# Linear attention and a squared-ReLU FFN in one kernel: the first batch's loads and its second group of rows, arranged anew

## The chip, the cores and the metric

The kernel runs on one core of a Trainium2 chip, in one launch. The metric is the device time of that launch in microseconds. The kernel before took 202.36 us in the median of three runs (202.26 to 202.84).

The core has five engines that run their own instructions in order and wait for each other by semaphores: TensorE (PE; its weight loads are shown apart as PEld), VectorE (DVE), ScalarE (ACT), GpSimd (POOL) and SyncE (SP, which issues most of the DMAs here; ACT issues a few). The DMAs of both queues run on the core's 16 DMA engines.

## The reference, cut to what matters

```python
# q, k, v: (4 batches, 4 heads, 1088 rows, 32); S1, S2: (8, 32); w_in: (128, 2048); w_out: (2048, 128)
def phi(x):                       # 64 features of a row: the outer product of two projections
    a = einsum('rd,bhsd->bhsr', S1, x)
    b = einsum('rd,bhsd->bhsr', S2, x)
    return einsum('bhsi,bhsj->bhsij', a, b).reshape(..., 64)
q_p, k_p = phi(q), phi(k)
kv  = einsum('bhsf,bhsd->bhfd', k_p, v)
z   = sum(k_p, axis=2)
num = einsum('bhsf,bhfd->bhsd', q_p, kv)
den = einsum('bhsf,bhf->bhs', q_p, z)[..., None] + 1e-06
x   = (num / den).transpose(0, 2, 1, 3).reshape(4352, 128)     # 4 heads side by side
out = maximum(x @ w_in, 0) ** 2 @ w_out                        # (4352, 128), float32
```

## The kernel before

**Tiling.** A batch has 1088 rows a head. A head's rows are laid over 32 partitions, 34 rows to a partition; the four heads of q or k fill the 128 partitions. The first 8 rows of 34 make tiles of group 0 and 1 (four tiles each), the last 2 rows are "the rest". v is laid the other way: partition 32 i + n holds rows 34 n + 8 i to 34 n + 8 i + 7, and the four heads stand side by side in the free dimension (256 numbers each), with a column of ones behind them. `load_v(b, i, eng)` fills 32 partitions (block i of rows) for all heads; four of them load a batch. `load_v_rest` loads the rest.

**The attention.** `turned` transposes q or k in 32 x 32 blocks on DVE; `proj` multiplies by S1 and S2 on PE and ACT copies the result out of PSUM; `outer` makes the 64 features of a row on DVE or POOL. `Kv` sums k's features times v over all rows (32 products of 128 rows and 4 of the rest) and `finish` copies the sums into the block-diagonal tile kvbd. `feature_t` transposes q's features on PE (t_ps) and copies them out (phT). `numerators` multiplies them by kvbd (nd). `normalize` divides on DVE by the denominators, scales each row for float16, transposes it on PE (x_ps) and has ACT copy it to xT: one chunk of 512 rows. Batches 1 to 3 go another way for some of this (`proj4`, `factors_gen`, `features_gen`, `KvRows`), where q's projections are written to a scratch in HBM (q_rows) and read back spread out (f, L285 and L290).

**The FFN.** Per chunk of 512 rows there are 16 blocks. A block multiplies xT by 128 columns of w_in (pg, L857), takes max(.,0) (gt) and squares it (g) on DVE, ACT and POOL, and multiplies by w_out (po, L944). `first_product` issues the first half some three blocks ahead of the second. There are 8 chunks, and a ninth of 256 rows made of the rests, whose products (po and po_r, L903) are made row block by row block; `rows_store` scales and stores them.

**Order.** The schedule is written by hand: instructions stand on each engine in the order in which the program issues them. The last part of the function, from the first `idle_products(6)` to `add_work`, is the first stretch: it makes chunk 0 and part of chunk 1 in straight line. After it a loop issues one block at a time, and between blocks `pump` lets generators ("lanes") issue pieces of the attention of later chunks: `x_gen` (numerators and normalization), `batch_gen`, `second_gen`. `now` counts blocks. `take_nd` and `nd_taken` guard the one PSUM buffer nd. Later loads are issued from a list by block number.

**PSUM buffers** are tagged: ms, pg and po have two buffers each, nd one. `idle_products` are products of zeros on PE, with no use of their result.

**DMA issue.** In the program's order, SP loads k's two groups and rest, q's group 0 (`load_group`), v (four `load_v`), q's group 1, w_in, w_out and then batch 1. Eight semaphores serve the DMAs in turn, so that an issue waits until the DMA eight places ahead of it has landed.

Of the kernel before, what the change touches and what calls it, by code (L numbers as in the profile page):

```python
# [21 lines left out]
def kernel(  # L22
# [86 lines left out]

    def load_v(b, i, eng):  # L110
        eng.dma_start(
            _v(v_sb[b], 0, [[256, H], [1, 256]], 32 * i, 32),
            bass.AP(
                v.tensor,
                v.offset + (b * H * S + 8 * i) * D,
                [[NM * D, 32], [S * D, H], [1, 256]],
            ),
        )

# [84 lines left out]
    own_j = cpool.tile([128, 16], F32)  # L204

    def sum_constants():
        dve.tensor_reduce(
            out=pick_s[:, :], in_=_v(iden, 0, [[1, 32], [32, 4]]), axis=AX, op=add
        )
        dve.tensor_copy(  # L210
            out=_v(pick, 0, [[8, 32], [1, 8]]), in_=_v(pick_s, 0, [[1, 32], [0, 8]])
        )
        dve.tensor_reduce(
            out=_v(own_j, 0, [[8, 2], [1, 8]]),
            in_=_v(iden, 0, [[64, 2], [1, 8], [8, 8]]),
            axis=AX,
            op=add,
        )
# [290 lines left out]
            )  # L509
        return nd  # L510

    def normalize(nd, T, xT, col, parts=1):

        small = [apool.tile([128, 16], F32, name=f"small{i}", tag=f"small{i}") for i in range(5)]
        den, rden, top, rtop, rs = small
        mm = apool.tile([128, 4], F32, tag="mm")
        mp = apool.tile([128, 4], F32, tag="mp")
        rm = apool.tile([128, 4], F32, tag="rm")
        beta = apool.tile([128, 4], F32, tag="beta", bufs=4)
        xs = apool.tile([128, 512], F16, tag="xs")  # L520
        num = _v(nd, 0, [[256, T], [VW, 4], [1, 32]])
        dve.tensor_scalar(
            out=den[:, 0 : 4 * T], in0=_v(nd, D, [[256, T], [VW, 4]]),
            scalar1=1e-6, scalar2=None, op0=add,
        )
        dve.reciprocal(rden[:, 0 : 4 * T], den[:, 0 : 4 * T])
        dve.tensor_reduce(
            out=_v(top, 0, [[4, T], [1, 4]]), in_=num,
            axis=AX, op=amax, apply_absolute_value=True,
        )  # L530
        yield 1, 1
        dve.tensor_tensor(
            out=rtop[:, 0 : 4 * T], in0=top[:, 0 : 4 * T], in1=rden[:, 0 : 4 * T], op=mult
        )
        dve.tensor_reduce(
            out=mm[:, 0:T], in_=_v(rtop, 0, [[4, T], [1, 4]]),
            axis=AX, op=amax, apply_absolute_value=True,
        )
        dve.tensor_scalar(  # L539
            out=mp[:, 0:T], in0=mm[:, 0:T], scalar1=1.0, scalar2=1.0 / 1024.0,  # L540
            op0=add, op1=mult,
        )
        dve.reciprocal(rm[:, 0:T], mp[:, 0:T])
        if parts == 1:
            dve.tensor_tensor(
                out=_v(rs, 0, [[4, T], [1, 4]]),
                in0=_v(rden, 0, [[4, T], [1, 4]]),
                in1=_v(rm, 0, [[1, T], [0, 4]]),
                op=mult,
            )  # L550
            yield 1, 1
            dve.tensor_tensor(
                out=_v(xs, 0, [[128, T], [32, 4], [1, 32]]),
                in0=_v(nd, 0, [[256, T], [VW, 4], [1, 32]]),
                in1=_v(rs, 0, [[4, T], [1, 4], [0, 32]]),
                op=mult,
            )
        else:
            yield 1, 1
            for i in range(T):  # L560
                dve.scalar_tensor_tensor(
                    out=_v(xs, 128 * i, [[32, 4], [1, 32]]),
                    in0=_v(nd, 256 * i, [[VW, 4], [1, 32]]),
                    scalar=rm[:, i : i + 1],
                    in1=_v(rden, 4 * i, [[1, 4], [0, 32]]),
                    op0=mult,
                    op1=mult,
                )
        pool.tensor_tensor(  # L569
            out=beta[:, 0:T], in0=mp[:, 0:T], in1=mp[:, 0:T], op=mult  # L570
        )
        yield 2, 0
        m = T if parts == 1 else 2
        for i in range(0, T, m):
            ms_used()
            x_ps = pspool.tile([128, 512], F16, name="x_ps", tag="ms", bufs=2)
            for t in range(i, i + m):
                nc.tensor.transpose(
                    x_ps[:, 128 * t : 128 * t + 128],
                    xs[:, 128 * t : 128 * t + 128],  # L580
                    iden16[:, :],
                )
            act.copy(
                xT[:, col + 128 * i : col + 128 * (i + m)], x_ps[:, 128 * i : 128 * (i + m)]
            )
        return beta
# [49 lines left out]
            yield 1, 0  # L636
        nd_taken[0] = True

    def x_gen(b, g, phT, rests=()):

        yield from take_nd()
        while pool_free[0] > now[0] + 0.6 and not hurry[0]:
            yield 1, 0
        nd = numerators(b, phT)
        quiet[0] = now[0] + 3
        yield 1, 1
        xT = apool.tile([128, 512], F16, name="xT", tag="xT", bufs=3)
        norm = normalize(nd, 4, xT, 0)
        yield next(norm)
        yield next(norm)  # L650
        next(norm)
        yield 1, 0
        nd_taken[0] = False
        for u in rests:
            rest_numerators(u)
        yield 1, 0
        yield from ms_one()
        beta = yield from norm
        chunk_of(b, g, xT, beta)
# [76 lines left out]
        if b % 2 == 1:  # L736
            add_work(rest_x(b // 2))

    def first_gen(phT):
        yield from x_gen(0, 1, phT)  # L740

    xT_rem = cpool.tile([128, 256], F16)
    rem_beta, rem_dst = [], []
    nd_rem, phT_rem = {}, {}
# [28 lines left out]
    def rest_x(r):  # L773
        beta = yield from normalize(nd_rem[r], 1, xT_rem, 128 * r)
        rem_beta.append((beta, 1))
        for w in range(2):
            for i in range(2):
                dst = bass.AP(
                    out.tensor,
                    out.offset + ((2 * r + w) * S + 32 + i) * E,  # L780
                    [[NM * E, 32], [1, E]],
                )
                rem_dst.append((dst, 64 * w + 32 * i, 32, 128 * r, 128))
        if r == 1:
            chunks[2 * B] = (xT_rem, 2, rem_beta, rem_dst)

# [124 lines left out]
    def rows_store(r, ci):  # L911
        beta, _ = chunks[ci][2][r]
        o_sb = fpool.tile([128, 128], F32, name="o_row", tag="o_row", bufs=2)
        dve.tensor_tensor(
            out=o_sb[:, :],
            in0=po[r][:, 0:128],
            in1=_v(beta, 0, [[0, 128]]),
            op=mult,
        )
        for i, (dst, p0, n, _, w) in enumerate(chunks[ci][3][4 * r : 4 * r + 4]):  # L920
            (sp, act)[i % 2].dma_start(dst, _v(o_sb, 0, [[1, w]], p0, n))

    def block():
        while len(stream) <= LOOK and first_product():
# [5 lines left out]
        if nt < 512:  # L930
            if c == 0:
                po[1] = pspool.tile([128, 512], F32, name="po_r", tag="ms", bufs=2)
            rows_product(c, 0, g2)
            if c < NC - 3:
                rows_product(c, 1, g2)
            else:
                held.append((c, 1, g2))
# [29 lines left out]
    xk += [turned(k_sb[0], g) for g in (1, 2)]  # L967
    pk = [proj(xk[0], "pg"), proj(xk[1], "pg")]
    proj_rests([(xk[2], 0, "k")])
    phk = [ph_tile("ph_k", 3) for g in range(2)]  # L970
    phq = ph_tile("ph_q", 2)
    for g in range(2):
        outer(phk[g], pk[g][1], 0, 2, dve, pk[g][0])
        outer(phk[g], pk[g][1], 2, 2, pool)
    xq = turned(q_sb[0], 0)
    idle_products(4)
    pq = proj(xq)
    outer_rest(0, "k", dve)
    outer(phq, pq[1], 0, 2, dve, pq[0])
    outer(phq, pq[1], 2, 1, dve, pq[0])  # L980
    outer(phq, pq[1], 3, 1, pool)
    xq1 = turned(q_sb[0], 1)
    sum_constants()
    kv0 = Kv(0)
    for g in range(2):
        kv0.tiles(phk[g], g, range(4))
    kv0.rest()
    kv0.finish((act, act))
    pqT = [feature_t(phq, 4, pr, (act, dve)[pr]) for pr in range(2)]
    nd0 = numerators(0, pqT, True)  # L990
    pq1 = proj(xq1, "pg")
    phq1 = ph_tile("ph_q", 2)
    for c in range(3):
        act.copy(
            w_in[:, 512 * c : 512 * c + 512], w_in32[:, 512 * c : 512 * c + 512]
        )
    idle_products(12)
    xT0 = apool.tile([128, 512], F16, name="xT", tag="xT", bufs=3)
    norm = normalize(nd0, 4, xT0, 0, 4)
    for _ in range(3):  # L1000
        next(norm)
    for t0 in (0, 2):
        outer(phq1, pq1[1], t0, 2, dve)
    try:
        next(norm)
    except StopIteration as done:
        chunk_of(0, 0, xT0, done.value)
    first_two()
    pqT1 = [feature_t(phq1, 4, pr, None) for pr in range(2)]
    for _ in range(2):  # L1010
        first_product()
    for pr in range(2):
        act.copy(pqT1[pr][0][:, :], pqT1[pr][1][:, :])
    act.copy(w_in[:, 1536:2048], w_in32[:, 1536:2048])

    lanes.append([first_gen([x[0] for x in pqT1]), 3, 1])
    add_work(*(batch_gen(b) for b in range(1, B)))
    later = []  # L1020
    for b in range(2, B):
# [45 lines left out]
```

## Time and profile before

| what | us |
|---|---|
| median of 3 runs | 202.36 |
| the profiled execution, its whole time | 202.01 |
| its span (first to last instruction) | 200.2 |
| PE busy | 193.0 |
| DVE busy | 121.9 |
| ACT busy | 109.4 |
| POOL busy | 62.7 |
| start of the first product with w_in (L886) | 17.86 |
| start of the first product with w_out (L944) | 19.68 |
| start of the last o_row on DVE (L914) | 196.80 |

The profile is of one execution. An engine's busy time is the time under its instructions; matmuls overlap in the pipeline, so PE's is not time at its peak. The chain of waits is followed back from the last instruction, at each step to what released it. "L245" is line 245 of the kernel before; tile names stand as output<-input. A window's row gives, for a stretch from A to B, the length, the busy us of PE, PEld, DVE, ACT and POOL with the instructions in brackets, the granted TensorE clock, the DMA share and GB/s.

### The profile page before, as it was taken

How to read it: one execution, taken by the hardware profiler on the slowest of the kernel's cores; microseconds unless marked ns; L12 is line 12 of the kernel's file. 1: busy time of each engine (PE TensorE's matmuls, PEld its weight loads, DVE VectorE, ACT ScalarE, POOL GpSimd, SP SyncE). 2: the span in 40 equal slices, each digit the busy share in tenths (PEclk: the TensorE clock that was granted, in tenths of full speed). 3: DMA queues.
4: the chain of work that ended last, by engine and by line, in shares of the span. 5: the costliest groups of instructions: out<-in, count | busy, mean ns of one | idle time of the engine just before them, and what ended most of it. 6: DMA issues, size and time to landing. Idle time of an engine off the chain costs nothing.

```text
span 200.2 us, 3760 instructions
## 1 busy us (share of the span) xinstructions
PE 193.0 (96%) x1416; PEld 102.8 (51%) x1416; DVE 121.9 (61%) x271; ACT 109.4 (55%) x216; POOL 62.7 (31%) x82
## 2 busy tenths in 40 slices
PE   7798999999999999999999999999999999999992
PEld 2575455455445464564346555454455444444792
DVE  4768694644994717459966573648456844544671
ACT  2236757544565566354674554555647565565570
POOL 3502220844262207441262254331332222223000
PEclk9999999999999999999999999999999999999999
DMA  5999720488300245782000117501000200100021
GB/s 159 279 356 246 229 47 0 137 188 211 111 0 0 66 153 164 210 246 81 2 3 0 52 58 222 194 3 54 0 0 3 52 0 0 38 16 0 3 52 26
DMA packets 14994, 18.34 MB, mean 92 GB/s; under 512 B 3072, under 2 KB 9472, under 8 KB 14976
## 3 DMA queue, kind: packets, MB, share of 16 engines
q1 hardware_dynamic: 14416, 18.00, 32.1%
q8 instruction: 11, 0.18, 0.4%
q10 hardware_dynamic: 560, 0.11, 0.3%
q14 instruction: 7, 0.06, 0.1%
HBM read 15.08 MB, written 3.01 MB: 90 GB/s over the span
## 4 chain that ended last, share of the span: by engine, by line
PE 86%; DVE 6%; DMA 4%; issue 1%; ACT 1%; SPq 0%; DVEq 0%
PE po L944 50%; PE pg L857 15%; PE nd L245 5%; DVE gt L873 2%; DMA v_sb<-in_v_dram 2%; PE kvr_ps L412 2%; PE o_ps L823 2%; PE ab_ps L245 2%; DMA k_sb<-in_k_dram 2%; PE po_r L903 2%; PE po L903 2%; PE idle_ps L224 1%; PE ab_ps L262 1%; PE kv_ps L375 1%; DVE ph_k L321 1%
## 5 line engine op out<-in xcount | busy, mean ns | idle before, releaser
L944 PE MATMUL po<-g,w_o 128*128 128x512 f32 x256 | 130.7, 592 | 0.0
L873 DVE TENSOR_SCALAR gt<-pg 128x512 f32<-128x512 f32 (+1 forms) x108 | 69.1, 646 | 51.7 <-PE pg L857 40.5
L876 ACT ACTIVATE g<-gt 128x512 f32<-128x512 f32 (+1 forms) x108 | 64.2, 599 | 66.0 <-DVE gt L873 63.7
L944 PEld LDWEIGHTS po<-g,w_o 128*128 128x128 f32 x256 | 48.5, 191 | 35.6 <-issue 21.3
L865 POOL TENSOR_TENSOR g<-gt 128x512 f32<-128x512 f32 x27 | 28.1, 1041 | 79.7 <-ACT gt L864 79.5
L857 PE MATMUL pg<-xT,w_in 128*128 128x512 f16 x126 | 47.8, 381 | 0.6 <-DVE gt L873 0.6
L857 PEld LDWEIGHTS <-w_in 128*128 128x128 f16 x142 | 13.9, 98 | 24.0 <-issue 22.8
L300 POOL TENSOR_TENSOR phT<-f,f 128x512 f32<-128x512 f32 x12 | 15.2, 1276 | 8.2 <-DMA f<-q_rows 8.2
L864 ACT ACTIVATE gt<-pg 128x512 f32<-128x512 f32 x27 | 15.9, 588 | 0.0
L321 POOL TENSOR_TENSOR ph_k<-ab 128x512 f32<-128x512 f32 x8 | 9.7, 1236 | 5.9 <-ACT ab L269 4.7
L245 PEld LDWEIGHTS nd<-kvbd,phT 128*64 128x64 f32 x256 | 8.3, 137 | 5.3 <-issue 4.0
L321 DVE TENSOR_TENSOR ph_k<-ab 128x512 f32<-128x512 f32 x6 | 6.2, 1036 | 6.5 <-ACT ab L269 6.5
L245 PE MATMUL nd<-kvbd,phT 128*64 128x66 f32 x256 | 9.5, 225 | 0.2 <-ACT phT L72 0.2
L569 POOL TENSOR_TENSOR beta<-mp 128x4 f32<-128x4 f32 (+1 forms) x10 | 2.1, 206 | 21.0 <-DVE mp L539 21.0
L224 PE MATMUL idle_ps<-zero 128*128 128x512 f16 x23 | 7.1, 455 | 1.2 <-DVE own L185 1.2
L829 DVE TENSOR_TENSOR o_sb<-o_ps,beta 128x512 f32<-128x512 f32 x8 | 5.5, 692 | 4.5 <-PE o_ps L823 2.7
L245 PEld LDWEIGHTS ab_ps<-w_bd,xt 128*64 128x64 f32 x160 | 6.2, 139 | 3.0 <-DVE xt L234 1.5
L245 PE MATMUL ab_ps<-w_bd,xt 128*64 128x64 f32 x160 | 6.4, 225 | 0.8 <-DVE xt L234 0.7
L234 DVE STREAM_TRANSPOSE xt<-k_sb 128x512 f32<-128x512 f32 x8 | 5.5, 698 | 1.7 <-DMA k_sb<-in_k_dram 1.7
L903 PE MATMUL po<-w_o,g 128*128 128x128 f32 x32 | 6.2, 280 | 0.1
L823 PEld LDWEIGHTS o_ps<-iden,oT 128*128 128x128 f32 x32 | 4.0, 141 | 3.7 <-issue 2.9
L903 PE MATMUL po_r<-w_o,g 128*128 128x128 f32 x32 | 5.9, 275 | 0.0
(110 smaller groups left out, 150.8 us busy)
## 6 DMA issues: line engine op xcount, KB each, us to landing
f<-q_rows SPq DMA_DIRECT2D x12, 256.0 KB
f<-q_rows SPq DMA_DIRECT2D x24, 128.0 KB
v_sb<-in_v_dram SPq DMA_DIRECT2D x16, 128.0 KB
out_dram<-o_sb SPq DMA_DIRECT2D x32, 64.0 KB
k_sb<-in_k_dram SPq DMA_DIRECT2D x3, 544.0 KB
q_sb<-in_q_dram SPq DMA_DIRECT2D x3, 544.0 KB
w_in<-in_moe_w_in_dram SPq DMA_DIRECT2D x2, 512.0 KB
w_o<-in_moe_w_out_dram SPq DMA_DIRECT2D x2, 512.0 KB
```

The costliest lines, as they stand in the source:

```text
L224: nc.tensor.matmul(idle_ps[:, :], zero[:, 0:128], zero[:, :])
L245: nc.tensor.matmul(out_ps[p0 + c : p0 + c + z, c0 : c0 + w], lhsT[:, l0 + c : l0 + c + z], rhs)
L300: eng.tensor_tensor(out=sb[:, :], in0=fs[0][:, :], in1=fs[1][:, :], op=mult)
L321: eng.tensor_tensor(out=_v(ph, 256 * t0, [[64, 4 * m], [8, 8], [1, 8]]), in0=_v(a, c0, [[n, 4 * m], [1, 8], [0, 8]]), in1=_v(b, c1, [[n, 4 ...
L823: nc.tensor.transpose(o_ps[:, 128 * t : 128 * t + 128], oT[:, 128 * t : 128 * t + 128], iden[:, :])
L857: nc.tensor.matmul(pg[:, 0:nt], w_in[:, 128 * c : 128 * c + 128], xT[:, 0:nt])
L864: act.activation(gt[:, 0:nt], pg[:, 0:nt], Relu)
L865: pool.tensor_tensor(out=g2[:, 0:nt], in0=gt[:, 0:nt], in1=gt[:, 0:nt], op=mult)
L873: dve.tensor_scalar(out=gt[:, 0:nt], in0=pg[:, 0:nt], scalar1=0.0, scalar2=None, op0=amax)
L876: act.activation(g2[:, 0:nt], gt[:, 0:nt], Square)
L903: nc.tensor.matmul(po[r][:, 0:128], g2[:, 128 * r : 128 * r + 128], w_o[:, 128 * c : 128 * c + 128], start=c == 0, stop=c == NC - 1,)
L944: nc.tensor.matmul(po[0][:, 0:nt], w_o[:, 128 * c : 128 * c + 128], g2[:, 0:nt], start=(c == 0), stop=(c == NC - 1),)
```

## The change

- `load_v` takes a head instead of a block of rows: it fills all 128 partitions with one head's 256 numbers. Its source pattern in HBM is now 4 blocks (8 rows apart) x 32 places x 256 numbers, where it was 32 places x 4 heads x 256 numbers.
- In the first stretch, q's group 0 is turned ahead of k's outer products on DVE; q's group 1 is turned behind kv's products. There are 17 idle products in all, where there were 23.
- The second group of batch 0: its projection stands ahead of the first group's numerators, its outer products are made by POOL (before: DVE, behind the normalization), its transposes stand among the idle products, ACT and DVE copy one half each of its features, and its numerators (nd1) stand right behind the first two products with w_in. `x_gen` takes nd1 and begins with the normalization. `normalize` gets the PSUM tag for x_ps as an argument, and uses po there, as ms holds the transposed features.
- `sum_constants` becomes a lane from block 8; its copy goes to POOL.
- The ninth chunk: a store covers 64 rows by a pattern of 2 x 32 rows (two stores per row block, one on SP and one on ACT), where four covered 32 each; two products of the second row block are held to the end, where three were.

```diff
--- before.py
+++ after.py
@@ -109,11 +109,11 @@
 
     def load_v(b, i, eng):
         eng.dma_start(
-            _v(v_sb[b], 0, [[256, H], [1, 256]], 32 * i, 32),
+            _v(v_sb[b], 256 * i, [[1, 256]]),
             bass.AP(
                 v.tensor,
-                v.offset + (b * H * S + 8 * i) * D,
-                [[NM * D, 32], [S * D, H], [1, 256]],
+                v.offset + (b * H + i) * S * D,
+                [[256, 4], [NM * D, 32], [1, 256]],
             ),
         )
 
@@ -204,10 +204,12 @@
     own_j = cpool.tile([128, 16], F32)
 
     def sum_constants():
+        yield 1, 0
         dve.tensor_reduce(
             out=pick_s[:, :], in_=_v(iden, 0, [[1, 32], [32, 4]]), axis=AX, op=add
         )
-        dve.tensor_copy(
+        yield 1, 0
+        pool.tensor_copy(
             out=_v(pick, 0, [[8, 32], [1, 8]]), in_=_v(pick_s, 0, [[1, 32], [0, 8]])
         )
         dve.tensor_reduce(
@@ -509,7 +511,7 @@
             )
         return nd
 
-    def normalize(nd, T, xT, col, parts=1):
+    def normalize(nd, T, xT, col, parts=1, ps_tag="ms"):
 
         small = [apool.tile([128, 16], F32, name=f"small{i}", tag=f"small{i}") for i in range(5)]
         den, rden, top, rtop, rs = small
@@ -573,7 +575,7 @@
         m = T if parts == 1 else 2
         for i in range(0, T, m):
             ms_used()
-            x_ps = pspool.tile([128, 512], F16, name="x_ps", tag="ms", bufs=2)
+            x_ps = pspool.tile([128, 512], F16, name="x_ps", tag=ps_tag, bufs=2)
             for t in range(i, i + m):
                 nc.tensor.transpose(
                     x_ps[:, 128 * t : 128 * t + 128],
@@ -636,12 +638,13 @@
             yield 1, 0
         nd_taken[0] = True
 
-    def x_gen(b, g, phT, rests=()):
-
-        yield from take_nd()
-        while pool_free[0] > now[0] + 0.6 and not hurry[0]:
-            yield 1, 0
-        nd = numerators(b, phT)
+    def x_gen(b, g, phT, rests=(), nd=None):
+
+        if nd is None:
+            yield from take_nd()
+            while pool_free[0] > now[0] + 0.6 and not hurry[0]:
+                yield 1, 0
+            nd = numerators(b, phT)
         quiet[0] = now[0] + 3
         yield 1, 1
         xT = apool.tile([128, 512], F16, name="xT", tag="xT", bufs=3)
@@ -736,9 +739,6 @@
         if b % 2 == 1:
             add_work(rest_x(b // 2))
 
-    def first_gen(phT):
-        yield from x_gen(0, 1, phT)
-
     xT_rem = cpool.tile([128, 256], F16)
     rem_beta, rem_dst = [], []
     nd_rem, phT_rem = {}, {}
@@ -774,13 +774,12 @@
         beta = yield from normalize(nd_rem[r], 1, xT_rem, 128 * r)
         rem_beta.append((beta, 1))
         for w in range(2):
-            for i in range(2):
-                dst = bass.AP(
-                    out.tensor,
-                    out.offset + ((2 * r + w) * S + 32 + i) * E,
-                    [[NM * E, 32], [1, E]],
-                )
-                rem_dst.append((dst, 64 * w + 32 * i, 32, 128 * r, 128))
+            dst = bass.AP(
+                out.tensor,
+                out.offset + ((2 * r + w) * S + 32) * E,
+                [[E, 2], [NM * E, 32], [1, E]],
+            )
+            rem_dst.append((dst, 64 * w, 64))
         if r == 1:
             chunks[2 * B] = (xT_rem, 2, rem_beta, rem_dst)
 
@@ -917,8 +916,8 @@
             in1=_v(beta, 0, [[0, 128]]),
             op=mult,
         )
-        for i, (dst, p0, n, _, w) in enumerate(chunks[ci][3][4 * r : 4 * r + 4]):
-            (sp, act)[i % 2].dma_start(dst, _v(o_sb, 0, [[1, w]], p0, n))
+        for i, (dst, p0, n) in enumerate(chunks[ci][3][2 * r : 2 * r + 2]):
+            (sp, act)[i % 2].dma_start(dst, _v(o_sb, 0, [[1, 128]], p0, n))
 
     def block():
         while len(stream) <= LOOK and first_product():
@@ -931,7 +930,7 @@
             if c == 0:
                 po[1] = pspool.tile([128, 512], F32, name="po_r", tag="ms", bufs=2)
             rows_product(c, 0, g2)
-            if c < NC - 3:
+            if c < NC - 2:
                 rows_product(c, 1, g2)
             else:
                 held.append((c, 1, g2))
@@ -967,55 +966,68 @@
     xk += [turned(k_sb[0], g) for g in (1, 2)]
     pk = [proj(xk[0], "pg"), proj(xk[1], "pg")]
     proj_rests([(xk[2], 0, "k")])
+    xq = turned(q_sb[0], 0)
     phk = [ph_tile("ph_k", 3) for g in range(2)]
     phq = ph_tile("ph_q", 2)
     for g in range(2):
         outer(phk[g], pk[g][1], 0, 2, dve, pk[g][0])
         outer(phk[g], pk[g][1], 2, 2, pool)
-    xq = turned(q_sb[0], 0)
-    idle_products(4)
+    idle_products(1)
     pq = proj(xq)
+    idle_products(1)
     outer_rest(0, "k", dve)
     outer(phq, pq[1], 0, 2, dve, pq[0])
     outer(phq, pq[1], 2, 1, dve, pq[0])
     outer(phq, pq[1], 3, 1, pool)
-    xq1 = turned(q_sb[0], 1)
-    sum_constants()
     kv0 = Kv(0)
     for g in range(2):
         kv0.tiles(phk[g], g, range(4))
     kv0.rest()
+    xq1 = turned(q_sb[0], 1)
     kv0.finish((act, act))
     pqT = [feature_t(phq, 4, pr, (act, dve)[pr]) for pr in range(2)]
-    nd0 = numerators(0, pqT, True)
     pq1 = proj(xq1, "pg")
     phq1 = ph_tile("ph_q", 2)
+    for t0 in (0, 2):
+        outer(phq1, pq1[1], t0, 2, pool)
+    nd0 = numerators(0, pqT, True)
     for c in range(3):
         act.copy(
             w_in[:, 512 * c : 512 * c + 512], w_in32[:, 512 * c : 512 * c + 512]
         )
-    idle_products(12)
+    tq1 = [pspool.tile([128, 512], F32, name="t_ps", tag="ms", bufs=2) for pr in range(2)]
+    pqT1 = [apool.tile([128, 512], F32, name="phT", tag=f"phT{pr}", bufs=2) for pr in range(2)]
+    for t0 in (0, 2):
+        idle_products((4, 3)[t0 // 2])
+        for pr in range(2):
+            for t in (t0, t0 + 1):
+                nc.tensor.transpose(
+                    tq1[pr][:, 128 * t : 128 * t + 128],
+                    phq1[:, 256 * t + 128 * pr : 256 * t + 128 * pr + 128],
+                    iden[:, :],
+                )
+    act.copy(pqT1[0][:, :], tq1[0][:, :])
+    idle_products(1)
     xT0 = apool.tile([128, 512], F16, name="xT", tag="xT", bufs=3)
-    norm = normalize(nd0, 4, xT0, 0, 4)
+    norm = normalize(nd0, 4, xT0, 0, 4, "po")
     for _ in range(3):
         next(norm)
-    for t0 in (0, 2):
-        outer(phq1, pq1[1], t0, 2, dve)
+    dve.tensor_copy(out=pqT1[1][:, :], in_=tq1[1][:, :])
     try:
         next(norm)
     except StopIteration as done:
         chunk_of(0, 0, xT0, done.value)
     first_two()
-    pqT1 = [feature_t(phq1, 4, pr, None) for pr in range(2)]
+    nd1 = numerators(0, pqT1, True)
+    nd_taken[0] = True
     for _ in range(2):
         first_product()
-    for pr in range(2):
-        act.copy(pqT1[pr][0][:, :], pqT1[pr][1][:, :])
     act.copy(w_in[:, 1536:2048], w_in32[:, 1536:2048])
 
 
 
-    lanes.append([first_gen([x[0] for x in pqT1]), 3, 1])
+    lanes.append([x_gen(0, 1, None, (), nd1), 3, 1])
+    lanes.append([sum_constants(), 8, 0])
     add_work(*(batch_gen(b) for b in range(1, B)))
     later = []
     for b in range(2, B):
```

## The prediction

> **What bounds the kernel now.** I read the page's shares and its chain of waits first.
>
> ```profile
> span 200.2 us, 3760 instructions
> PE 193.0 (96%) x1416; PEld 102.8 (51%) x1416; DVE 121.9 (61%) x271; ACT 109.4 (55%) x216; POOL 62.7 (31%) x82
> PE 86%; DVE 6%; DMA 4%; issue 1%; ACT 1%; SPq 0%; DVEq 0%
> ```
>
> TensorE sets the end: once its products with w_in start it hardly stops. So the change is worth what it does to three places: the stretch before the first product with w_in, what stands in PE's row afterwards, and the last stores. Next I read the chain in order of time for the first 24 us (start, length, work).
>
> ```profile
> 1.26 3.42 DMA k_sb<-in_k_dram
> 4.70 4.07 DMA v_sb<-in_v_dram
> ...
> 8.90 2.46 PE kv_ps L375 x72
> 11.36 0.60 PE t_ps L490 x4
> 11.99 0.59 ACT phT L72
> 12.62 1.23 PE nd L245 x32
> 13.86 0.47 PE ab_ps L245 x16
> 14.32 2.69 PE idle_ps L224 x12
> 17.17 0.66 ACT xT L583 x2
> 17.86 0.59 PE pg L886 x2
> 18.45 0.87 PE t_ps L490 x8
> 19.33 0.43 PE pg L857 x2
> 19.76 1.05 PE po L944 x2
> 22.96 1.08 PE nd L245 x31
> ```
>
> The arrival of batch 0's v starts everything: 8.90 to 17.86 (8.96 us) is one chain from it. I therefore counted the trace's own DMA records, packet by packet and semaphore step by step. v is 512 packets of 1 KB, the first at 4.86; they took 46 ns while few were under way, 64.5 on average (68 after 5.5). Its four loads landed at 7.22, 7.76, 8.25 and 8.87, each in 16 steps, one for each DMA engine. q's first group, just ahead, landed in 16 steps from 5.21 to 6.66.
>
> **The change, part by part.**
>
> *v head by head (L111).* Bytes and packets stay. The pattern on the HBM side had 32 as its outermost count; now it has 4 (four blocks of 8 rows). Not every load in the trace comes in 16 steps: the two loads of S (outermost 8) come in 8 steps after one jump of eight, and so does L285, whose source has 8 outermost though its tile has 64 partitions. L290 (16 outermost) comes in 16. Where little but L285 is under way, about half the DMA engines work:
>
> ```profile
> 41.90:42.40 0.50, 0.50 (x3) 0.38 (x2) 0.20 (x1) 0.26 (x1) 0.00 (x0) 1.00 0.57 94
> 81.50:82.00 0.50, 0.50 (x2) 0.00 (x0) 0.47 (x1) 0.00 (x0) 0.00 (x0) 1.00 0.47 111
> ```
>
> (The last two columns are the DMA share and GB/s.) The engines follow the smaller outermost count, so I take 4 for v; the other end is 16. With 4, one engine carries 128 packets instead of 32. It comes free of q at about 5.4 (median step 5.8 less 0.4). Per packet I take 55 ns, between 46 and 64.5, since the other 12 engines go on with w_in: 128 x 55 = 7.0. With 0.45 to land: 12.85, against 8.87: **+4.0**. Ends: 46 ns gives 11.75 (+2.9); 76 ns, the mean of batch 1's v packets while other loads ran, gives 15.6 (+6.7). Heads don't help: the fourth product already needs head 3.
>
> The Trainium skill (DMA: Bandwidth & Descriptors, "Why a DMA increments its semaphore by 16 and not by 1", and its rule "Use all 16 engines") says that a DMA runs on the largest number up to 16 that divides the slowest counts of both its patterns; it gives 4 here and 2 for the new stores, so the same sum; the 8-step loads agree.
>
> *q turned ahead of k's outer products.* DVE then waits for q until 6.66: 6.66 + 0.70 (L234) + 1.47 (two outers) = 8.83, against 7.30 before. Behind it are outer_rest, q's outers and kv. With v at 12.85 it costs nothing; with v at 8.87, nothing either, by 0.04.
>
> *Fewer idle products* (23 to 17, 0.23 each) leave PE still from about 8.3 to 12.9. No stretch like it is in the trace, except the start: the first six idle products took 2.74, where twelve later took 2.76, so 1.36 lost after a still PE. The kv products, 2.46, could lose as much as themselves. Ends 0 and 2.5; I take the start's own, **+1.3**.
>
> The Trainium skill (TensorE: Matmul & The Clock Gate, Part 1) has the clock halve after an idle window of some 3.4 us, and return after as much work; that would cost at most 1.7 here. The granted clock reads 1.00 even under the six slow products, so no row here shows it directly.
>
> *Second group's features early.* q's second group lands behind v on those four engines (32 packets x 27 ns, 0.9 later) and is turned (0.70) 1.8 us before DVE's phT copy needs DVE: hidden. Its projection now stands ahead of the numerators: 0.47, of which 0.24 fills PE's wait for phT: **+0.25** (ends 0 and 0.5). POOL makes the outers, 2 x 1.04 (1.24 if slowed, as in its later rows), done 2 us after the projection, under the 2.9 us of 7 idle products, 8 transposes and the last idle one. ACT copies phT (0.59) ahead of the two xT copies (0.66); that ends 4.03 after nd0, against 4.00: **+0.03**.
>
> *Second group's numerators early.* The nd at 22.96 leaves the stream (-1.09) and stands where the transposes were at 18.45 (1.09 for 0.87): **-0.87**. The slot exists because the first po waits for g anyway. Ends -1.09 and -0.3 (if DVE's copy of phT, 0.69, comes late).
>
> *Moved into the stream:* the sum constants (DVE 0.34 and 0.39, a POOL copy); DVE idles 39%, so nothing; 0.7 if it had none to spare.
>
> *v of batches 1 to 3* also runs on four engines. After v0 (12.4) these carry q 0.9, w_in 2.6, w_o 3.4, k1 1.3, v1 7.0, then q1 1.35: it lands at 29.4. DVE turns q1 at 28.24, plus the 4.7 by which the stream is late: 3.5 us spare. SP waits longer in front of v1 (6.20 us for its four issues before); behind it in SP's row are q1, k2, v2 and the q_rows store. v2 is through at about 37.9, q_rows goes at 34.71 + 4.7: 1.5 spare. Uncovered, DVE or PE waits one for one.
>
> *The last stores.* Two per row block instead of four. The chain ends so:
>
> ```profile
> 195.60 0.49 PE po L903 x2
> 196.09 0.69 PE po_r L903 x6
> 196.80 0.29 DVE o_row L914
> ```
>
> Eight stores then issue until 198.2, and the last landed at 199.49. The new ones have 2 outermost in HBM: 4 x 64 packets of 512 B on two engines are 128 each, x 27 ns = 3.46. From the first packet at 197.15 that ends at 200.6, lands at 200.95: **+1.46**. Ends -0.6 (16 engines, fewer issues) and +2.0. Holding two po_r products instead of three (-0.23) is hidden behind these.
>
> **Sum:** 4.0 + 1.3 + 0.25 + 0.03 - 0.87 + 1.46 = +6.2. The profiled execution took 202.01 (span 200.2, 1.8 around it), 0.35 under the median 202.36. Added to the two: 208.2 and 208.5; I say 208.4.
>
> **Rivals.**
>
> 1. *All 16 engines serve the new loads and stores.* For: same bytes, a tile of all 128 partitions. Against: L285, where a wide tile didn't help. v then lands before 8.87, DVE's 8.83 decides, kv starts at 8.9; PE is never still: 0.28 - 0.87 - 0.6 = -1.2, **201.2**, faster. It decides if v0's steps are 16.
> 2. *Narrow, but mild:* packets at 46 ns or less, PE at full speed, stores overlapping (+0.7): 2.4 + 0.28 - 0.87 + 0.7 = +2.5, **204.9**. For: 46 ns is what few packets at a time took.
> 3. *The backlog reaches batch 1.* At 76 ns v2 ends near 45.5, q_rows would go at 43; phT then misses its nd, which PE reaches 1.05 us after phT is ready (47.41, 48.46): a stall of 1.5. 6.7 + 1.3 + 0.28 - 0.87 + 1.46 + 1.5 = +10.4, **212.7**. For: POOL waits for f already (1.9 at most).
>
> **Chances.** Forecast 0.72 (205.4 to 211.5), rival 1 0.08, rival 2 0.10, rival 3 0.10. The range 204.3 to 212.5 holds the forecast's cases and most of rival 2. A measurement can't tell less than 0.3% from no change. Faster 0.07, same 0.01 (between rivals 1 and 2), slower 0.92.
>
> **What would show it.** Right: v0's loads in 4 steps, the chain held by v_sb until 12 to 14; the first kv products slower than 34 ns a pass; no nd near the third po; the stores after the last o_row longer than 3 us. Wrong at the root: v0 in 16 steps, or kv starting near 9.

## The result, and the profile after

| | before | after |
|---|---|---|
| median of 4 runs each, us | 202.45 (202.26 to 202.84) | 210.22 (209.20 to 211.17) |
| the profiled execution, us | 202.01 | 211.17 |
| its span | 200.2 | 209.4 |

The ratio is 1.038 (95% interval 1.033 to 1.043): slower by 7.8 us, where +6.0 was forecast (208.4 against 202.36). Medians and ratios leave out slow runs, those more than 1.5% above the fastest run of the same kernel; among all the runs here there is one. The profiled execution of after is the longest of its four, so a sum over its trace has to give 9.14 us (to two decimals the spans are 209.36 and 200.22), not 7.8.

The page of after, its head, PE's shares, the row of the granted clock in 40 slices and the shares of the chain of waits:

```profile
span 209.4 us, 3741 instructions
...
PE 195.2 (93%) x1410; PEld 104.8 (50%) x1410; DVE 124.1 (59%) x271; ACT 109.3 (52%) x215; POOL 64.2 (31%) x83
...
PEclk9958999999999999999999999999999999999996
...
PE 73%; DVE 8%; issue 6%; DMA 4%; POOL 4%; SPq 2%; ACT 2%; POOLq 0%; DVEq 0%; ACTq 0%
```

PE's busy time grew by 2.2 us though six idle products are gone; the 5 in the clock's third slice says where. Some 7 of the 9.1 us are time in which PE stands. The chain of after in order of time (start, length, work):

```profile
4.84 7.78 DMA v_sb<-in_v_dram
...
12.66 4.09 PE kv_ps L377 x66
16.75 1.44 PE t_ps L492 x8
18.18 0.61 PE ab_ps L247 x16
18.80 0.94 PE nd L247 x32
19.73 0.97 PE idle_ps L226 x4
...
23.52 0.38 ACT xT L585
23.95 0.59 PE pg L885 x2
24.54 1.08 PE nd L247 x32
25.62 0.54 PE pg L856 x2
26.16 0.86 PE po L943 x2
```

v_sb holds the chain until 12.62, the kv products behind it take 62 ns a pass (4.09 / 66) where they took 34 (2.46 / 72), and the first product with w_in starts at 23.95, 6.09 later than before.

To place the rest, I took the start of each block's second product with w_out (po) in both traces and subtracted. The lag is +6.21 in blocks 0 to 2 and +5.02 from block 3, as nd no longer stands there. (It dips for some blocks, by up to 2.5, where a piece of the attention now stands a block or more later in PE's order; those dips close again.) Between blocks 43 and 51 it rises to +6.67, falls back to +5.90 by block 58, steps to +6.44 at 63 and to +6.71 at 93, and stays. So the stretch after block 3 lost 1.69 again. From the start of the first o_row to the span's end, 4.09 (196.13 to 200.22) became 6.52 (202.84 to 209.36):

```profile
202.84 0.29 DVE L913 TENSOR_TENSOR o_row<-po,beta 128x128 f32<-128x128 f32 x1 [1.03 <-PE po L902]
203.16 1.23 SPq L920 DMA_DIRECT2D out_dram<-o_row  x2
203.16 1.49 ACTq L920 DMA_DIRECT2D out_dram<-o_row  x2
203.29 0.29 DVE L913 TENSOR_TENSOR o_row<-po_r,beta 128x128 f32<-128x128 f32 x1 [0.15 <-PE po_r L902]
```

Those are after's last instructions (a timeline: start, length, engine, line, work, and what the engine waited for). Behind them lie only the stores. The sum: 6.21 - 1.19 + 1.69 + 2.43 = 9.14.

### The profile page after: what moved, and what is told of

Same layout as the page of the kernel before. It is cut to its first block, busy times and chain, and to the rows that moved or that the text cites. A ratio compares the mean times of both kernels' runs of the same rounds, so it can differ in the third digit from the quotient of the medians.

```text
span 209.4 us, 3741 instructions
## 1 busy us (share of the span) xinstructions
PE 195.2 (93%) x1410; PEld 104.8 (50%) x1410; DVE 124.1 (59%) x271; ACT 109.3 (52%) x215; POOL 64.2 (31%) x83
## 4 chain that ended last, share of the span: by engine, by line
PE 73%; DVE 8%; issue 6%; DMA 4%; POOL 4%; SPq 2%; ACT 2%; POOLq 0%; DVEq 0%; ACTq 0%
PE po L943 39%; PE pg L856 12%; PE nd L247 4%; DVE gt L872 4%; DMA v_sb<-in_v_dram 4%; POOL phT L302 2%; PE kv_ps L377 2%; DVE ph_k L323 2%; PE kvr_ps L414 2%; PE po L902 2%; PE o_ps L822 2%; PE ab_ps L247 2%; PE po_r L902 2%; PE ab_ps L264 1%; PE x_ps L580 1%
## 5 line engine op out<-in xcount | busy, mean ns | idle before, releaser
L872 DVE TENSOR_SCALAR gt<-pg 128x512 f32<-128x512 f32 (+1 forms) x110 | 70.5, 648 | 55.8 <-PE pg L856 47.4
L875 ACT ACTIVATE g<-gt 128x512 f32<-128x512 f32 (+1 forms) x110 | 65.4, 599 | 67.2 <-DVE gt L872 64.6
L864 POOL TENSOR_TENSOR g<-gt 128x512 f32<-128x512 f32 x25 | 26.0, 1039 | 75.6 <-ACT gt L863 75.6
L863 ACT ACTIVATE gt<-pg 128x512 f32<-128x512 f32 x25 | 14.7, 587 | 0.3 <-ACT phTr L760 0.2
L323 POOL TENSOR_TENSOR ph_k<-ab 128x512 f32<-128x512 f32 x8 | 10.3, 1298 | 12.3 <-ACT ab L271 11.3
L236 DVE STREAM_TRANSPOSE xt<-q_sb 128x512 f32<-128x512 f32 x8 | 5.6, 702 | 4.7 <-DMA q_sb<-in_q_dram 4.7
L377 PE MATMUL kv_ps<-v_sb,ph_k 128*64 128x64 f32 x64 | 4.6, 312 | 3.1 <-DMA v_sb<-in_v_dram 3.1
L226 PE MATMUL idle_ps<-zero 128*128 128x512 f16 x17 | 6.1, 470 | 1.2 <-DVE own L185 1.2
L323 DVE TENSOR_TENSOR ph_k<-ab 128x512 f32<-128x512 f32 x6 | 6.7, 1108 | 0.0
```

Of the source, the lines that this page charges most:

```text
L236: dve.transpose(xt[:, :], _v(x, 128 * g, [[32, 4], [256, 4], [1, 32]]))
L323: eng.tensor_tensor(out=_v(ph, 256 * t0, [[64, 4 * m], [8, 8], [1, 8]]), in0=_v(a, c0, [[n, 4 * m], [1, 8], [0, 8]]), in1=_v(b, c1, [[n, 4 ...
L377: nc.tensor.matmul(self.ps[x : x + z, 64 * (h // 2) : 64 * (h // 2) + 64], ph[p0 : p0 + n, c0 + 64 * h + f : c0 + 64 * h + f + z], _v(vt, ...
L863: act.activation(gt[:, 0:nt], pg[:, 0:nt], Relu)
L864: pool.tensor_tensor(out=g2[:, 0:nt], in0=gt[:, 0:nt], in1=gt[:, 0:nt], op=mult)
L872: dve.tensor_scalar(out=gt[:, 0:nt], in0=pg[:, 0:nt], scalar1=0.0, scalar2=None, op0=amax)
```

## The experiments

Medians are set beside those of the kernel before on the same chip: 202.68 (13 runs) for the first four, 202.65 (13 and 17 runs) for the others. Differences from after are taken from its 210.22 above, where before had 202.45; medians of before thus differ by 0.2 from place to place.

**One part undone: v by row blocks again.**

```diff
-            _v(v_sb[b], 256 * i, [[1, 256]]),
+            _v(v_sb[b], 0, [[256, H], [1, 256]], 32 * i, 32),
...
-                [[256, 4], [NM * D, 32], [1, 256]],
+                [[NM * D, 32], [S * D, H], [1, 256]],
```

> The changed kernel with v loaded by blocks of rows again (32 places outermost in HBM), nothing else. Theory (the new loads run on 4 DMA engines; the wait and the slow TensorE clock behind it are most of the loss): v0 lands in 16 steps near 8.9, the kv products start near 8.9 and run at 34 ns a pass, the first product with w_in stands near 18 instead of 23.95, and the time falls by 5 to 6.5 us from 210.2, to 203.7 to 205.2; the long tail of the last stores stays. Rival (the new order of the first stretch and the stream costs the time): the first product with w_in comes later than 20 and the time stays above 207.

Measured: 205.63 (205.06 to 207.85, 4 runs), ratio 1.016 (1.010 to 1.022): 4.6 less than after, a fall somewhat smaller than the 5 to 6.5 expected. kv starts at 9.17, its 72 products take 2.46 again (34 ns each), and the granted clock of the run is 0.992, where after's is 0.974. The slow kv products went with the late v. What kv waits for last here are DVE's outer products (0.17), which stand behind q's turning.

**The stores undone: four of 32 rows again.**

```diff
-        for i, (dst, p0, n) in enumerate(chunks[ci][3][2 * r : 2 * r + 2]):
+        for i, (dst, p0, n, _, w) in enumerate(chunks[ci][3][4 * r : 4 * r + 4]):
```

> The changed kernel with the four stores of 32 rows per row block again, the loads of v left narrow. Theory (the stores of 64 rows run on 2 DMA engines): from the last o_row to the end of the span 3.4 us instead of 6.1, the time falls by 2 to 3 us from 210.2, to 207.2 to 208.2. Rival (the tail is long for another reason, the last products or the held ones): no change beyond 0.5 us.

Measured: 208.25 (207.26 to 209.85, 4 runs), ratio 1.028 (1.023 to 1.033), 2.0 less than after. From its first o_row to the span's end it is 4.12 (202.35 to 206.47).

**Both undone: the new order alone** (both diffs above together).

> The changed kernel with the old loads of v and the old stores: what is left is the new order of the first stretch. Theory: a gain of about 1 us against the kernel before, 200.8 to 202.2, the second group's numerators gone from the stream (a lag by block that falls by 1.1 to 1.2 us at the third block), and what DVE and POOL lose in the stream by chance. Rival (the new order itself costs): slower than the kernel before, above 203.

Measured: 202.62 (202.26 to 203.65, 10 runs), ratio 1.000 (0.998 to 1.002). A gain to 200.8 to 202.2 was expected, and the median shows none: the order by itself is worth nothing that these runs can tell, and nearly the whole 7.8 lies in the two access patterns. The ten runs fall into two groups, six from 202.26 to 202.70 and four from 203.27 to 203.65; the profiled one, at 203.65, is of the second. In its trace kv starts only at 10.02, behind v. The run with v by row blocks, whose first stretch is the same, has kv at 9.17, and before with the new stores alone (below) has it at 9.60, where before has 8.90: with the same old loads, v lands up to 0.9 later in one execution than in another.

**One part alone: before with the new v loads.**

```diff
-                [[NM * D, 32], [S * D, H], [1, 256]],
+                [[256, 4], [NM * D, 32], [1, 256]],
```

> The kernel before with the new loads of v alone. Theory: v0 lands in 4 steps an engine near 12.6, kv starts about 3.8 us later and at half speed, 207 to 209.5 (4.5 to 7 us over before). Rival (the narrow loads hurt only together with the new order, for instance because DVE turns q first): less than 2.5 us over before.

Measured: 207.08 (205.67 to 207.83, 3 runs; a fourth, at 209.69, is left out), ratio 1.020 (1.015 to 1.026): +4.4. The run of 205.67 is the only one whose granted clock stayed at 1.00 throughout; the others have 0.982 to 0.987. So the clock does not fall in every run, and the one run without the fall is +3.0. In the trace (the run of 207.83) the lag is +5.82 in the first block and +5.82 in the last: the loads of batches 1 to 3, which use the same pattern, delay nothing.

**One part alone: before with the new stores** (the last hunks of the change, with two products held instead of three).

> The kernel before with the new stores of 64 rows alone (three products held, as before). Theory (2 DMA engines): each of the four stores lands in 2 steps, their packets take 3.4 us, and the end comes 2 to 2.6 us later: 204.4 to 205.2. Rival (the tail of the changed kernel belongs to its later products): within 0.5 us of 202.5.

Measured: 204.99 (204.95 to 205.14, 4 runs), ratio 1.012 (1.010 to 1.014): +2.34. From its first o_row to the span's end 6.52 (196.83 to 203.35), as in after.

**After with PE kept busy while v is on its way.**

```diff
     idle_products(1)
     pq = proj(xq)
-    idle_products(1)
+    idle_products(21)
```

> The changed kernel with 21 idle products instead of one ahead of the kv products, so that TensorE is busy until v arrives; nothing else. Theory (behind the wait for v TensorE's clock is halved): the granted clock stays at 1.00 in the first 20 us, the kv products take 34 ns a pass again, the first product with w_in comes 2 to 2.5 us earlier, the time falls from 210.2 to 207.5 to 208.5 and the runs lie closer together. Rival (the slow kv products wait for data, not for a clock): no change.

Measured: 208.50 (208.03 to 208.99, 4 runs), ratio 1.028 (1.025 to 1.031): 1.7 less than after, for twenty products more, and the runs lie within 1.0 us, where after's lie within 2.0. The granted clock is 1.00 from 8.00 to 14.80. The chain of this run, in order of time:

```profile
7.77 4.64 PE idle_ps L226 x21
12.41 2.39 PE kv_ps L377 x72
14.80 1.02 PE t_ps L492 x8
15.82 0.61 PE ab_ps L247 x16
```

v's last step is at 11.73 in this run, and the idle products hold kv until 12.41, so they are some 0.6 us too many. But all 72 kv products take 2.39 (33 ns each), and the eight transposes 1.02 instead of 1.44. The first product with w_in comes at 21.59 instead of 23.95: 0.25 from kv's earlier start, 1.70 from kv, 0.42 from the transposes.

**After with the sum constants made in the first stretch again** (and old loads and stores, as above).

```diff
+    for _ in sum_constants():
+        pass
...
-    lanes.append([sum_constants(), 8, 0])
```

> The changed kernel with the old loads and stores, and the sum constants made in the first stretch again instead of in a lane from block 8; TensorE's order in the stream is then that of the kernel before but for the early numerators. Theory (the lane takes turns from batch 1's generator, moves its pieces by a block, and that costs the stream 1.3 us at the 45th to 64th block): the gain of 1.2 us of the early numerators stays, 201.0 to 201.7. Rival (the stream loses because the second group's normalization starts earlier, with or without the lane): no change from 202.6.

Measured: 202.31 (201.71 to 203.81, 10 runs), ratio 0.998 (0.996 to 1.001). In the trace the lag is +0.07 from block 3 to block 92, with no step between 43 and 58, and +0.35 at the end. The two tables of what PE waited for in the stream (line, releaser, us in total, times, longest), first the new order alone, then this run:

```profile
PE pg L857 <- DVE gt L873: 0.5, 2, 0.3
...
PE nd L247 <- POOL phT L302: 0.3, 1, 0.3
```

```profile
PE pg L857 <- DVE gt L873: 0.4, 1, 0.4
```

Between blocks 3 and 92 the lag of the new order alone grows by 1.0 and this run's by nothing, while the waits differ by 0.4; the other 0.6 is named by no wait. Over these blocks PE stands 0.57 longer in the first of the two traces and is busy 0.44 longer, with 920 products in both; why the same products take longer is not shown. The medians differ by 0.31, less than the intervals can tell, and 201.0 to 201.7 was expected: neither the theory nor its rival is settled by them. What the traces say of it stands in the next section.

**After, head by head, but with the 32 places outermost in HBM.** A tile's partitions then stand in another order, and k's transposes write in the same order, so the sums are the same.

```diff
-                [[256, 4], [NM * D, 32], [1, 256]],
+                [[NM * D, 32], [256, 4], [1, 256]],
...
-                xt[:, :], _v(x, 128 * g, [[32, 4], [256, 4], [1, 32]])
+                _v(xt, 0, order), _v(x, 128 * g, [[32, 4], [256, 4], [1, 32]])
...
+    by_place = ((128, 4), (1, 4), (4, 32))
```

> The changed kernel, v still loaded head by head into 128 partitions, but with the 32 places outermost in HBM and the 4 blocks inside; k's rows are turned into the same order (the transposes of k write with a stride), so the sums are the same. Theory (the number of DMA engines follows the outermost count): v0 lands in 16 steps before 8.9, kv waits for DVE's outer products at 9.1, and the time is 204.8 to 205.8, the long tail left. Rival (loads of a head over 128 partitions are slow whatever the order): v0 after 11 and the time above 208.

Measured: 205.14 (204.46 to 205.87, 4 runs), ratio 1.012 (1.008 to 1.016), 5.1 less than after, with v's bytes and packets unchanged; apart from the loads only k's transposes differ, which are slower (below). Its chain:

```profile
5.81 5.35 DMA q_sb<-in_q_dram
11.19 0.72 DVE xt L236
...
11.95 0.69 PE ab_ps L249 x16
12.64 0.94 PE nd L249 x32
```

v_sb is out of the chain: kv starts at 8.12, sooner than the 9.1 expected, and what is waited for last is q's second group, which lands behind v at 11.16. In after this landing was hidden, as PE was still at its late kv products; here the projection "ahead of the numerators" has to wait for it.

**The best of the parts:** the wide head-by-head loads, the old stores, the constants in the first stretch.

```diff
-                [[256, 4], [NM * D, 32], [1, 256]],
+                [[NM * D, 32], [256, 4], [1, 256]],
...
+    for _ in sum_constants():
+        pass
...
+        for i, (dst, p0, n, _, w) in enumerate(chunks[ci][3][4 * r : 4 * r + 4]):
```

> The changed kernel with three things otherwise: v's loads have the 32 places outermost and the 4 blocks of rows inside (k's transposes write in the same strided order, so the sums are the same), the four stores of 32 rows are there again, and the constants for the sums are made in the first stretch. Theory (what the change lost are the narrow loads, the narrow stores and the batch 1 pieces moved by the constants; what it gained is nd1 early, 1.2): the first product with w_in at 17.8 to 18.1 as in the run with the wide loads, then a lag of about -1.1 from block 3 to the last block without a step at block 44, and 4.1 from the first o_row to the end of the span: 201.0 to 202.0, faster than before by 0.3 to 0.8%. Rival A (q's second group, which lands behind v, and the strided transposes eat the gain): first product with w_in at 18.4 or later, 202.3 to 203. Rival B (batch 1's pieces shift for another reason than the constants): the lag goes from -1.1 to about +0.1 at block 44, 202.2 to 202.7.

Measured: 202.17 (201.22 to 202.81, 12 runs), ratio 0.997 (0.995 to 0.999). It beats before by about 0.5 us, and misses the forecast of 201.0 to 202.0 by 0.2. The first product with w_in is at 18.00 and the lag -0.91 from block 3, near the theory's -1.1; then it steps to -0.56 at block 58 and to -0.26 at 93. At the first step PE waits for DVE, which is busy with a strided transpose of k (its eight take 1.07 to 1.19 each, where the eight of q take 0.67 to 0.71); a timeline of the stretch:

```profile
97.10 1.09 DVE L236 STREAM_TRANSPOSE xt<-k_sb 128x512 f32<-128x512 f32 x1
...
98.06 0.66 DVE L875 TENSOR_SCALAR gt<-pg 128x512 f32<-128x512 f32 x1
...
98.77 0.38 PE L859 MATMUL pg<-xT,w_in 128*128 128x512 f16 x1 [0.30 <-DVE gt L875]
```

So rival A had a part, in the stream and not at the start.

## Why the prediction was right, and where its sizes were off

**Four DMA engines for v: right.** By the trace's records of semaphore steps, each of batch 0's four loads in after makes one jump and then four steps: 7.04 to 8.03, 8.40 to 9.64, 10.10 to 11.09, 11.42 to 12.62. Forecast: 12.85. In part this was luck, as two errors cancelled: the packets took 46 ns in the median (48.5 in the mean), not 55, but the slowest of the four engines was already 0.98 behind the first in the first load and 1.2 in the last. Counted back from that first load's landing at 8.02 (32 packets of 46 ns, and 0.45 to land) it began at about 6.1, by my estimate, not at 5.4. The term was +4.0; kv's bulk starts 3.76 later (12.66, not 8.90). In the run with the 32 places outermost, each load comes in 16 steps and the last in at 8.35. Same bytes, same packets, same median of 46 ns; in the loads only the order of the two counts in HBM differs. Rival 1 (16 engines) fell with this. By the rule of the Trainium skill that the prediction cites (DMA: Bandwidth & Descriptors, "Why a DMA increments its semaphore by 16 and not by 1"), 4, 2 and 16 engines follow for the three patterns; the steps of all three agree.

**PE slow after standing still: right, and mis-sized.** +1.3 was the term. The kv products lost 4.09 - 66 x 0.0342 = 1.83, and the eight transposes 0.42 (1.44 against 1.02 in runs at full clock): 2.25 in all, for which the run with PE kept busy gave back 2.1 at the start and 1.7 in the median. The prediction took the size from the first idle products, 1.36; there the slow time began with the work. Here it began earlier and lasted longer. (The prediction read a clock of 1.00 under those first products; before's trace holds no record of the clock ahead of 4.82, so that 1.00 is no measurement.) Windows of after (stretch, length, PE, PEld, DVE, ACT and POOL busy, granted clock, DMA share, GB/s):

```profile
7.33:10.74 3.41, 1.59 (x21) 1.02 (x21) 2.50 (x6) 0.37 (x1) 1.16 (x2) 1.00 0.88 227
10.74:14.15 3.41, 1.96 (x30) 1.78 (x32) 0.71 (x1) 0.00 (x0) 0.00 (x0) 0.50 1.05 343
14.15:17.56 3.41, 3.41 (x48) 3.17 (x45) 0.00 (x0) 0.42 (x2) 0.00 (x0) 0.50 1.07 338
```

The clock was 0.50 from 10.74 to 17.57, 6.83 us; this covers kv's bulk from its start to its end (12.66 to 16.75) and more than half of the transposes (to 18.18). In the first of these stretches PE still ran 1.59 of 3.41 us, and that did not keep the clock; 1.96 in the second did not bring it back. The Trainium skill (TensorE: Matmul & The Clock Gate, Part 1) has free-running windows of 3.4 us; two of them would be the 6.83, and the bound of 1.7 that the prediction drew from that section left out that a window in which only the first heads' few products run need not count as busy. That last reading rests on three traces, each with 6.83 us at 0.50: after, before with the new loads (10.95 to 17.78) and after with the old stores (10.13 to 16.96). It was not tried by itself. How large the loss is hangs on where these stretches fall, which differs from run to run: one run of before with the new loads had no fall at all. So no size of this term could have been right for every run.

**The new order of the first stretch: right.** +0.28 was the term. With a clock that stays up, the way from kv's start to the first po grew by 0.41 (the run with constants in the first stretch). So, for the first po: 3.76 (kv starts its bulk at 12.66, not 8.90) + 1.63 (4.09 for 2.46) + 0.42 + 0.41 = 6.22, against a lag of 6.21. Turning q ahead cost nothing while v was late, as forecast. With an early v it does cost, where the prediction had "nothing either, by 0.04": v's chain in before ends at 8.77, not 8.87, so DVE's 8.83 comes last, and with v by row blocks kv starts at 9.17, behind DVE, 0.27 later than before.

**nd1 early: right, a little small.** -0.87 net was the term, of which 1.09 for the nd that leaves the stream; the lag falls by 1.17 to 1.20 at block 3 in the traces of all eight kernels with the new order.

**The sum constants "so nothing": the step that failed, in the traces.** "DVE idles 39%, so nothing; 0.7 if it had none to spare" asked whether DVE had time for three small operations. The price came by another way. The lane takes turns of the pump, and batch 1's and 2's pieces move back: in PE's order the projections of batch 1 stand in block 11 instead of 10, its kv products in 17 to 20 instead of 15 to 17, its numerators in 22 and 34 instead of 21 and 32; from block 57 on the order is the same. They then meet other work. One such place is seen in the timelines, first after, then before:

```profile
91.00 1.27 POOL L302 TENSOR_TENSOR phT<-f,f 128x512 f32<-128x512 f32 x1 [0.81 <-DMA f<-q_rows]
...
91.17 1.13 DVE L524 TENSOR_SCALAR small<-nd_rem 128x4 f32<-128x4 f32 x1
...
92.60 0.68 DVE L872 TENSOR_SCALAR gt<-pg 128x512 f32<-128x512 f32 x1
...
93.33 0.38 PE L856 MATMUL pg<-xT,w_in 128*128 128x512 f16 x1 [0.70 <-DVE gt L872]
```

```profile
84.60 0.17 DVE L522 TENSOR_SCALAR small<-nd_rem 128x4 f32<-128x4 f32 x1
```

The same operation takes 0.17 alone and 1.13 when it starts under POOL's phT, and gt stands late behind it: PE waits 0.70 for it, and at this block (49) the lag steps from +5.49 to +6.35. What the stream gained or lost, by the lags of each trace:

| kernel | lag at the first po | from block 3 | last block | lost in the stream |
|---|---|---|---|---|
| after | +6.21 | +5.02 | +6.71 | 1.69 |
| v by row blocks | +0.69 | -0.51 | +1.16 | 1.67 |
| old stores | +5.65 | +4.45 | +6.22 | 1.77 |
| new order alone | +1.53 | +0.33 | +1.63 | 1.30 |
| PE kept busy | +3.85 | +2.66 | +4.48 | 1.82 |
| 32 places outermost | +0.05 | -1.14 | +0.10 | 1.24 |
| new order, constants first | +1.26 | +0.07 | +0.35 | 0.28 |
| the best of the parts | +0.26 | -0.91 | -0.26 | 0.65 |
| before with new loads | +5.82 | +5.82 | +5.82 | 0 |
| before with new stores | +0.70 | +0.70 | +0.70 | 0 |

The first column holds v's landing too, which differs between executions (+0.70 in the last row, with before's own first stretch). All six traces with the lane lose 1.2 to 1.8 in the stream; of the four without, the two with nd1 early lose 0.28 and 0.65, the two with before's order nothing. So in these executions the lane eats what nd1 early brought. For the medians this is not shown: taking the lane out gave 0.31, inside the intervals. Whether the two groups of runs of the order alone, 1.0 apart, are runs with and without such meetings stays open, as only one of them has a trace.

**v of batches 1 to 3: right,** 0 by the steady +5.82; rival 3 (a stall in batch 1) fell with it.

**The last stores: right, and mis-sized.** +1.46 was the term; alone they cost +2.34 in the median, and 2.43 from the first o_row on in after. The data went as forecast: 27 ns a packet, each store one jump and two steps, 3.52 us from the first packet (204.40) to the end of the last (207.92), where 3.46 was forecast. Most of what was missing lies at the two ends. The first packet comes 1.24 us after the issue at 203.16. The prediction's 197.15 stands for 0.70; before's own trace has 0.81 (197.26), and so have all six traces with the old stores, within 0.02, where all five with the new ones have 1.24. Of the 0.43 more, 0.28 is the issue itself, which takes 0.59 instead of 0.31; why, and what the rest is, wasn't tried. From the last landing (208.25) to the span's end it is 1.11, where before has 0.84 (its last store landed at 199.38, not at 199.49): in after, SP still goes through five waits, some 0.065 apart, where one was left before. Against the term these are 0.54 + 0.06 + 0.27 + 0.11, near the missing 0.97.

**Rival 2** (204.9, PE at full speed, stores overlapping) had the packets' 46 ns right (in the median), and its other two conditions wrong in after's trace.

In the medians the parts, each alone on before, make +4.40 (loads) + 2.34 (stores) - 0.06 (order) = +6.7, of the 7.8 measured; taken out of after, loads and stores are worth 4.6 and 2.0. The rest of about 1.1 is no single part's, and no run was made for it.

## What to carry to other kernels

Read a DMA's width from its semaphore steps before changing its pattern: the same bytes with the 4 outside the 32 cost some 4 to 5 us here, and the 32 outside (with k's order changed to match) gave them back. If PE must wait for a load, the wait can cost twice, once as idle time and once in the products behind it; idle products over the whole wait gave back 1.7 us here. Work that an idle engine "has time for" need not be free when it takes a turn in a schedule: compare the order of the other pieces before and after, and look for where they meet another engine.

## What the runs showed of the hardware that was not expected

- In three of the eleven traces the granted clock fell to 0.50 for 6.83 us around kv, though PE had been busy 1.59 (after), 1.30 (before with the new loads) and 1.97 us (old stores) of the 3.41 us before. It came back only after a stretch that was full. PE's busy time alone does not decide it: the new order alone was busy 2.05 in such a stretch (4.45 to 7.86), and the run with PE kept busy 1.65 near its end (199.37 to 202.78), and both kept 1.00. What does decide it is open.
- A DVE operation of 128 x 4 numbers took 1.13 us instead of 0.17 and ended at 92.30, as POOL's phT did (92.27). Another (L534, 0.17 in the median) took 0.59 from 20.82 to 21.41, under POOL's outer products that end at 21.38. The Trainium skill (SBUF — State Buffer, "SBUF: two separate sides") has GpSimd and certain operations of DVE (those in a two-port mode, or with two inputs in SBUF) lock a shared pair of ports for a whole instruction; both ends agree with it. The change moved these outer products to POOL, and the prediction did not look for it.
- 1 KB packets of batch 0's v took 46 ns in the median into tiles of all 128 partitions, in all six such traces, over 4 engines as over 16. The loads into 32 partitions took 64 to 76 ns in the median in the other five, and v landed the later for it in some of them.
